# Attention weights of query tiles 3 and 4 normalised behind their exponentials instead of at the slot's end

## The chip, the cores and the metric

The kernel runs on one core of a Trainium2 chip, with float32 inputs and outputs. The metric is the device time of one execution in microseconds (us), measured without the profiler; before the change three runs gave a median of 985.2 us. A change of this kernel can be told from no change when it is over about 0.2%, some 2 us.

## What is computed

Three layers follow each other: causal attention with a memory term, a dense two-layer block, and a mixture of eight experts in which each token goes to one. The change lies in the attention alone:

```
scores = scale * np.matmul(q, k.transpose(0, 1, 3, 2))          # B, H, S, D = 4, 8, 576, 64
scores = np.where(causal, -1000000000.0, scores)
a = np.exp(scores - scores.max(-1, keepdims=True))
a /= a.sum(-1, keepdims=True) + 1e-09
local = np.matmul(a, v)
...
return (g * mem_out + (1 - g) * local).astype(np.float32)
```

The result, 2304 tokens by 512, goes through `(h * clip(h + 3, 0, 6) / 6) @ w_out` with `h = x @ w_in`, and then through the experts.

## The kernel before, in words

**Units of attention.** The 32 heads are worked on as 16 pairs (`Pair`, L261), two heads at a time. The 576 queries of a head are cut into five tiles, 0 to 4, the first of 64 queries and the others of 128; tile i sees 64, 192, 320, 448 or 576 keys. A pair goes through these steps, each a method with a letter:

- B, `start` (L301): VectorE writes the memory term of all tiles into the weights' tiles `a` (L314).
- S, `scores` (L319): TensorE multiplies `qd` and `kd` into PSUM tiles `pa` (L337); VectorE scales, masks and reduces them in one instruction with an accumulator read (L343), which gives `st` and the extreme `mn`. S0 does tiles 0 and 1 and a corner of 4; S2, S3 and S4 do one tile each.
- X, `exp` (L349): ScalarE takes the exponential into `a` and sums it into `sm` (L352), once for each head.
- N, `norm` (L355): VectorE adds up the sums (L360) and inverts them (L361), and GpSimd multiplies the weights by the inverse in place (L365). N0 does tiles 0, 1 and 2 of both heads, six instructions on GpSimd; N3 does tiles 3 and 4, four instructions.
- T, `turn` (L367): TensorE transposes the normalised weights by 128 x 128 blocks into `pa` (L376), and ScalarE (L91) or VectorE (L93) copies them to `aw`. TA and TB turn blocks of tiles 3 and 4, TC blocks of tiles 4, 2 and 1, TD of 0, 1 and 2.
- V, `values` (L381): TensorE multiplies `vt` by `aw` (L389), and ScalarE copies the result into `x`. V3 is tiles 3 and 4, V0 the others.
- M and L are the memory term and the loads of the pair after the next.

The `pa` tiles come from a pool of four PSUM buffers (L245).

**Slots.** `PROGRAM` (L75) is a string that is run 17 times, for t = -1 to 15; one run is a slot (`act`, L427). In slot t, the steps T and V are those of pair t, and B, S, X and N those of pair t + 1, so that one pair is turned while the next is scored. C and D load and convert a piece of the dense block's weights (`load64`, L135: a load of 512 KB, then L150 and L91 on ScalarE, L154, L155, L164 and L166 on VectorE). U asks for the next unit of the dense block (`mlp`, L168), whose matmuls are L213 and L182; there are none before slot 4, when the first 512 tokens are there. From slot 4 the dense block's units fill the slots.

**What sets the order.** Every engine works its instructions in the order in which the program gives them. The program text is not that order: a scheduler takes the instructions and places them on the engines by when it thinks their inputs are there, and, among those that are, by their place in the text. So the position of N3 in `PROGRAM` is a priority, and what becomes of it has to be looked up in the built program.

```
def norm(self, g):
    tiles = GROUPS[g]
    g0, g1 = tiles[0], tiles[-1] + 1
    for j in range(2):
        h, a, r = 2 * self.hp + j, self.a[j], self.rs[j]
        DVE.tensor_reduce(r[:, g0:g1], self.sm[j][:, g0:g1], axis=AX.X, op=ALU.add)
        DVE.reciprocal(r[:, g0:g1], r[:, g0:g1])
        for i in tiles:
            m, n, o = QN[i], QK[i], QO[i]
            av = a[:m, o + D : o + D + n]
            ENG[NORM[i]].tensor_scalar(av, av, r[:m, i], omg[:m, h : h + 1], op0=ALU.mult, op1=ALU.mult)
```

`GROUPS` (L259) is `{0: (0, 1, 2), 3: (3, 4)}`, and `NORM` is GpSimd for all five tiles.

Of the kernel before, what the change touches and what calls it, by code (L numbers as in the profile page):

```python
# [23 lines left out]
B, H, S, D = 4, 8, 576, 64  # L24
# [17 lines left out]
TB = 256  # L42
# [29 lines left out]
ET = {'A': mybir.EngineType.Activation, 'D': mybir.EngineType.DVE, 'P': mybir.EngineType.Pool, 'T': mybir.EngineType.PE}  # L72


PROGRAM = 'B S0 L TA S3 X0 U X3 X1 I U TB S4 C U X4 TC U S2 C X2 N0 M0 TD U M1 V3 N3 M2 D U K U M3 V0 U U'  # L75


def f32(ap):
# [4 lines left out]
def tile_kernel(ctx, tc, qT, kT, qn, vx, z, beta, w_in, w_out, w_gates, w1, w2, out):  # L83
# [343 lines left out]
    def act(t, x):  # L427

        nonlocal it
        pair = lambda n: pairs[n] if 0 <= n < len(pairs) else None  # L430
        k, n = x[0], int(x[1]) if x[1:].isdigit() else None
        cur, nxt, far = pair(t), pair(t + 1), pair(t + 2)
        if k == "U":
            other()
        elif k == "I":
            if t in ready:
                for _ in it:
                    pass
                it = mlp(ready[t], 0, end1)
                other()  # L440
        elif k == "L":
            if far:
                far.load()
        elif k == "K":
            if nxt and nxt is not pairs[0]:
                nxt.load_v()
        elif k in "CD":
            if conv and (k == "C" or t >= 3):
                load64(cv, 0, *conv.pop(0))
        elif k == "B":  # L450
            if nxt:
                nxt.start()
        elif k == "S":
            if nxt:
                nxt.scores(n)
        elif k == "X":
            if nxt:
                nxt.exp(n)
        elif k == "N":
            if nxt:  # L460
                nxt.norm(n)
        elif k == "T":
            if cur:
                cur.turn(x[1])
        elif k == "V":
            if cur:
                cur.values(n)
        elif k == "M":
            if far:
                far.memory(n)  # L470
# [4 lines left out]
    for t in range(-1, len(pairs)):  # L475
        for x in PROGRAM.split():
            act(t, x)
# [742 lines left out]
```

## Time and profile before

| | |
|---|---|
| median of 3 runs | 985.2 us (984.69 to 986.05) |
| the profiled execution | 991.04 us |
| its span, first to last instruction | 989.2 us |
| mean granted clock of TensorE over the span | 0.973 |
| TensorE (PE) busy | 917.4 us, 93% |
| VectorE (DVE) busy | 622.1 us, 63% |
| ScalarE (ACT) busy | 520.3 us, 53% |
| GpSimd (POOL) busy | 367.7 us, 37% |

PE stands for matmuls and PEld for weight loads, which overlap them. A busy share is an average over the whole kernel, and TensorE's matmuls are pipelined, so a full TensorE need not be at its peak. In the timelines a line gives the start, the time, the engine, the line of the kernel, the operation with its output and input, how many were merged, and in brackets the idle time in front of it with what ended it. The granted clock is a share of full speed: 1.00 is 2.4 GHz, 0.50 is 1.2 GHz.

### The profile page before, as it was taken

What the parts mean: (1) busy time and instruction counts of PE and PEld (TensorE: products, weight loads), DVE (VectorE), ACT (ScalarE), POOL (GpSimd) and SP (SyncE); (2) the same over time, 40 slices, a digit from 0 to 9 for tenths busy, and PEclk for the clock granted to TensorE, in tenths of its full rate; (3) what the DMA queues carried; (4) which work ended last, traced back from release to release, by engine and by line L of the source; (5) the groups of instructions that cost most, each with busy time, mean ns of one, the idle gap of its engine ahead of it and who ended that gap; (6) DMA issues with size and microseconds to landing.
All of it is one profiled execution on the core that took longest, in us unless ns stands there. A gap on an engine that the chain in (4) does not pass through costs nothing. (4 is left out here: it accounts for less than half of the span.)

```text
span 989.2 us, 17067 instructions
## 1 busy us (share of the span) xinstructions
PE 917.4 (93%) x5733; PEld 720.5 (73%) x5733; DVE 622.1 (63%) x1511; ACT 520.3 (53%) x1084; POOL 367.7 (37%) x574
## 2 busy tenths in 40 slices
PE   4677799999999999899999999999887999999996
PEld 2344477777776777788888888888766778778875
DVE  6766797565657541778344444447767668678982
ACT  5556666565546543445222222223346668768883
POOL 1543376445546552435533333335221123112210
PEclk9987799999999999989999999999999999999998
DMA  6432332221213010543011111112323565532850
GB/s 196 129 100 95 118 117 71 76 75 54 75 54 100 14 35 17 176 129 128 22 44 44 43 44 43 45 43 107 107 76 118 204 240 190 204 130 104 319 201 23
DMA packets 49278, 101.70 MB, mean 103 GB/s; under 512 B 5341, under 2 KB 15581, under 8 KB 49184
## 3 DMA queue, kind: packets, MB, share of 16 engines
q1 hardware_dynamic: 45696, 89.74, 26.8%
q0 software_dynamic: 3488, 10.80, 3.2%
q8 instruction: 47, 0.77, 0.3%
q14 instruction: 47, 0.39, 0.1%
HBM read 136.66 MB, written 14.72 MB: 153 GB/s over the span
## 5 line engine op out<-in xcount | busy, mean ns | idle before, releaser
L646 DVE TENSOR_TENSOR wL<-st,wH 128x1024 fp32r<-128x1024 f32 x136 | 163.7, 1227 | 43.2 <-ACT wH L641 37.5
L213 PE MATMUL hps<-xH,wH 128*128 128x256 f32 x576 | 166.8, 290 | 1.6 <-ACT xH L91 1.4
L213 PE MATMUL hps<-xL,wH 128*128 128x256 f32 x576 | 162.2, 282 | 2.9 <-DVE xL L200 2.9
L95 POOL TENSOR_SCALAR gH<-g 128x256 fp32r<-128x256 f32 x144 | 63.6, 441 | 271.8 <-DVE g L217 214.4
L365 POOL TENSOR_SCALAR a<-a,rs,omg 128x320 f32<-128x320 f32 (+4 forms) x160 | 126.9, 805 | 97.1 <-DVE rs L360 72.5
L213 PE MATMUL hps<-xH,wL 128*128 128x256 f32 x576 | 161.2, 280 | 0.0
L217 DVE SCALAR_TENSOR_TENSOR g<-g,hps 128x256 f32<-128x256 f32 x144 | 60.0, 417 | 146.4 <-ACT g L216 146.4
L641 ACT CAST wH<-st 128x1024 fp32r<-128x1024 f32 x136 | 139.7, 1053 | 8.5 <-DMA st<-w 8.4
L216 ACT ACTIVATE g<-hps,half 128x256 f32<-128x256 f32 x144 | 68.0, 472 | 137.4 <-PE hps L213 112.3
L213 PEld LDWEIGHTS hps<-xH,wH 128*128 128x128 f32 x576 | 108.9, 189 | 18.6 <-issue 12.6
L221 POOL TENSOR_TENSOR gL<-g,gH 128x256 fp32r<-128x256 f32 x144 | 115.4, 802 | 11.8
L213 PEld LDWEIGHTS hps<-xL,wH 128*128 128x128 f32 x576 | 109.1, 189 | 8.6 <-DVE xL L200 3.8
L352 ACT ACTIVATE a<-st,mn 64x64 f32<-64x64 f32 (+4 forms) x160 | 88.4, 555 | 48.0 <-DVE mn L343 48.0
L376 PE MATMUL pa<-ident,a 128*128 128x128 f32 (+1 forms) x480 | 81.9, 302 | 32.1 <-POOL a L365 28.5
L213 PEld LDWEIGHTS hps<-xH,wL 128*128 128x128 f32 x576 | 109.1, 190 | 0.1
L376 PEld LDWEIGHTS pa<-ident,a 128*128 128x128 f32 (+1 forms) x480 | 59.0, 151 | 60.6 <-POOL a L365 33.8
L182 PE MATMUL acc<-wH,gH 128*128 128x512 f32 x288 | 95.5, 413 | 1.3 <-POOL gH L95 1.2
L182 PE MATMUL acc<-wH,gL 128*128 128x512 f32 x288 | 91.7, 400 | 2.3 <-POOL gL L221 2.3
L337 PE MATMUL pa<-kd,qd 64*128 64x64 f32 (+5 forms) x384 | 83.7, 488 | 10.3 <-DVE mn L343 5.4
L182 PE MATMUL acc<-wL,gH 128*128 128x512 f32 x288 | 91.0, 397 | 0.0
L343 DVE CUSTOM_DVE_ANT_0 st<-pa,mask 64x64 f32<-64x64 f32 (+4 forms) x160 | 52.9, 372 | 33.0 <-PE pa L337 33.0
L182 PEld LDWEIGHTS acc<-wH,gL 128*128 128x128 f32 x288 | 54.2, 190 | 16.2 <-POOL gL L221 3.5
(239 smaller groups left out, 1674.6 us busy)
## 6 DMA issues: line engine op xcount, KB each, us to landing
st<-w SPq DMA_DIRECT2D x136, 512.0 KB
sw<-w SPq DMA_DIRECT2D x32, 512.0 KB
w<-w_in SPq DMA_DIRECT2D x16, 512.0 KB
w<-w_out SPq DMA_DIRECT2D x16, 512.0 KB
qnt<-qn SPq DMA_DIRECT2D x16, 320.0 KB
vt<-vx SPq DMA_DIRECT2D x16, 320.0 KB
x2d<-row SPq DMA_DIRECT2D x18, 258.0 KB
qd<-qT SPq DMA_DIRECT2D x16, 288.0 KB
```

The lines of the kernel that those rows point to most:

```text
L95: POOL.tensor_scalar(out, x, 1.0, 1.0, op0=ALU.mult, op1=ALU.mult)
L182: PE.matmul(acc[t], lhsT=gg[:, t * P : (t + 1) * P], rhs=ww[:, 512:1024], start=m == 0 and first, stop=m == HM - 1 and last)
L213: PE.matmul(hps, lhsT=ww[:, kk * P : (kk + 1) * P], rhs=xx[:, kk], start=k == 0, stop=k == 3 * KD - 1)
L216: ACT.activation(g, hps, AF.Relu, bias=half, scale=1.0 / 6.0)
L217: DVE.scalar_tensor_tensor(g, g, 1.0, hps, op0=ALU.min, op1=ALU.mult)
L221: ENG[GL].tensor_tensor(gL, g, f32(gH), op=ALU.subtract)
L337: PE.matmul(pss[j][: QN[i], o : o + k1 - k0], lhsT=self.qd[r, QS[i] : QS[i] + QN[i]], rhs=self.kd[r, k0:k1], start=True, stop=True)
L352: ACT.activation(self.a[j][:m, o + D : o + D + n], self.st[j][i][:m, :n], AF.Exp, bias=self.mn[j][:m, i : i + 1], scale=-1.0, accum_out=se ...
L365: ENG[NORM[i]].tensor_scalar(av, av, r[:m, i], omg[:m, h : h + 1], op0=ALU.mult, op1=ALU.mult)
L376: PE.transpose(psa[:, off : off + QN[i]], self.a[j][: QN[i], QO[i] + c * P : QO[i] + (c + 1) * P], ident[: QN[i], : QN[i]])
L641: ACT.copy(self.H[c], stage[c])
L646: DVE.tensor_tensor(self.L[c], stage[c], f32(self.H[c]), op=ALU.subtract)
```

## The change

One token of `PROGRAM` moves: N3 stood behind V3, near the slot's end, and now stands behind X4, the exponentials of tile 4, and in front of TC. Nothing is added or removed.

```
-PROGRAM = 'B S0 L TA S3 X0 U X3 X1 I U TB S4 C U X4 TC U S2 C X2 N0 M0 TD U M1 V3 N3 M2 D U K U M3 V0 U U'
+PROGRAM = 'B S0 L TA S3 X0 U X3 X1 I U TB S4 C U X4 N3 TC U S2 C X2 N0 M0 TD U M1 V3 M2 D U K U M3 V0 U U'
```

What the built program makes of it is shown at two places, both in slot 1, in which pair 2 is scored; the later numbers in names tell buffers apart.

On GpSimd, before: `a_464` and `a_465` are the weights of pair 2's two heads, and the memsets prepare the sums of pair 4.

```order
L365 TENSOR_SCALAR a_465<-a_465,rs_471,omg 128x320
L308 MEMSET sm_856 128x10
L308 MEMSET sm_857 128x10
L309 MEMSET sm_856 128x1
L309 MEMSET sm_857 128x1
L365 TENSOR_SCALAR a_464<-a_464,rs_470,omg 128x448
L365 TENSOR_SCALAR a_464<-a_464,rs_470,omg 128x576
L365 TENSOR_SCALAR a_465<-a_465,rs_471,omg 128x448
L365 TENSOR_SCALAR a_465<-a_465,rs_471,omg 128x576
```

GpSimd with the change, the same pair:

```order
L365 TENSOR_SCALAR a_464<-a_464,rs_470,omg 128x448
L365 TENSOR_SCALAR a_464<-a_464,rs_470,omg 128x576
L365 TENSOR_SCALAR a_465<-a_465,rs_471,omg 128x448
L365 TENSOR_SCALAR a_465<-a_465,rs_471,omg 128x576
L308 MEMSET sm_856 128x10
L309 MEMSET sm_856 128x1
L365 TENSOR_SCALAR a_464<-a_464,rs_470,omg 64x64
```

The four instructions of N3 (448 and 576 keys) stood behind the six of N0; now they stand in front of them.

On VectorE, before: `rs` are the inverted sums, 128x3 those of N0 and 128x2 those of N3; `w` and `wL` belong to the conversion of the dense block's weights, `phi` and `pz` to the memory term of pair 3.

```order
L360 TENSOR_REDUCE rs_470<-sm_468 128x3
L93 COPY aw<-pa 128x320
L361 RECIPROCAL rs_470<-rs_470 128x3
L360 TENSOR_REDUCE rs_471<-sm_469 128x3
L292 SCALAR_TENSOR_TENSOR phi<-qnt,phi 128x640
L166 TENSOR_TENSOR wL_555<-w_588,wH_554 128x512
L361 RECIPROCAL rs_471<-rs_471 128x3
L360 TENSOR_REDUCE rs_470<-sm_468 128x2
L360 TENSOR_REDUCE rs_471<-sm_469 128x2
L295 TENSOR_TENSOR pz<-phi,zb 128x10x64
L361 RECIPROCAL rs_470<-rs_470 128x2
L361 RECIPROCAL rs_471<-rs_471 128x2
```

VectorE with the change, from the end of tile 4's scores to the first of tile 2's:

```order
L343 ISA st_483,mn_467<-pa,mask,mn 128x512
L343 ISA mn_467 128x1
L155 SCALAR_TENSOR_TENSOR w_556<-w_556 128x512
L360 TENSOR_REDUCE rs_470<-sm_468 128x2
L154 TENSOR_SCALAR w_596<-w_596 128x512
L164 SCALAR_TENSOR_TENSOR w_556<-w_556 128x512
L361 RECIPROCAL rs_470<-rs_470 128x2
L360 TENSOR_REDUCE rs_471<-sm_469 128x2
L93 COPY aw<-pa 128x512
L361 RECIPROCAL rs_471<-rs_471 128x2
L343 ISA st,mn_466<-pa,mask 128x320
L343 ISA mn_466 128x1
```

The sums of N3 were added up and inverted behind those of N0 and all scores of the slot; now this happens between the scores of tile 4 and those of tile 2, in between the steps of a weight conversion. TensorE's order is the same but for single matmuls of the dense block in slot 0. From slot 5 on, the orders of all engines are the same before and after, and there N3 stands in front of N0 in both.

## Rows read from the trace of the kernel before

**Rows 1.** The page: the span, and busy time of each engine.

```profile
span 989.2 us, 17067 instructions
PE 917.4 (93%) x5733; PEld 720.5 (73%) x5733; DVE 622.1 (63%) x1511; ACT 520.3 (53%) x1084; POOL 367.7 (37%) x574
```

**Rows 2.** Waits of PE, 0 to 125 us: us in total, times, longest.

```profile
PE pa L376 <- POOL a L365: 26.9, 17, 7.2
```

**Rows 3.** Waits of PE, 120 to 400 us: the same wait.

```profile
PE pa L376 <- POOL a L365: 1.6, 2, 0.9
```

**Rows 4.** Slots 0, 2, 5-15: length; PE, PEld, DVE, ACT, POOL busy; clock; DMA; GB/s.

```profile
28.90:49.70 20.80, 16.14 (x87) 9.21 (x87) 15.02 (x52) 12.51 (x32) 9.18 (x15) 1.00 0.34 114
...
71.03:92.02 20.99, 15.46 (x87) 8.90 (x87) 15.05 (x53) 13.25 (x34) 8.16 (x15) 0.84 0.35 114
...
140.00:400.00 260.00, 257.94 (x1755) 194.38 (x1754) 151.47 (x509) 142.07 (x390) 135.54 (x235) 1.00 0.20 63
```

**Rows 5.** Timeline of PE, end of slot 1 and most of slot 2.

```profile
66.34 1.02 PE L337 MATMUL pa<-kd,qd 64*64 64x64 f32 x12
71.03 0.33 PE L376 MATMUL pa<-ident,a 128*128 128x128 f32 x1 [3.67 <-POOL a L365]
71.84 1.17 PE L376 MATMUL pa<-ident,a 128*128 128x128 f32 x4 [0.48 <-POOL a L365]
73.34 0.90 PE L376 MATMUL pa<-ident,a 128*128 128x128 f32 x3 [0.33 <-POOL a L365]
74.17 1.87 PE L337 MATMUL pa<-kd,qd 64*128 64x448 f32 x4
75.97 1.97 PE L376 MATMUL pa<-ident,a 128*128 128x128 f32 x8
77.87 1.58 PE L337 MATMUL pa<-kd,qd 64*128 64x512 f32 x4
79.38 1.10 PE L376 MATMUL pa<-ident,a 128*128 128x128 f32 x8
```

**Rows 6.** Timeline of POOL: N0 and N3 of slot 1, N3 of slots 4 and 8.

```profile
65.20 4.72 POOL L365 TENSOR_SCALAR a<-a,rs,omg 64x64 f32<-64x64 f32 x6 [13.21 <-DVE rs L360]
...
70.14 3.15 POOL L365 TENSOR_SCALAR a<-a,rs,omg 128x448 f32<-128x448 f32 x4
...
140.39 4.75 POOL L365 TENSOR_SCALAR a<-a,rs,omg 128x448 f32<-128x448 f32 x4
...
222.41 3.03 POOL L365 TENSOR_SCALAR a<-a,rs,omg 128x448 f32<-128x448 f32 x4 [1.34 <-DVE rs L361]
```

**Rows 7.** Timeline of DVE: its long waits in slots 0, 2 and 4, and tile 4's scores in slot 8.

```profile
29.93 0.43 DVE L154 TENSOR_SCALAR w<-w 128x512 int32<-128x512 int32 x1 [0.63 <-DMA w<-w_out]
35.06 0.62 DVE L343 CUSTOM_DVE_ANT_0 st<-pa,mask 128x448 f32<-128x448 f32 x1 [4.09 <-PE pa L337]
...
76.07 0.62 DVE L343 CUSTOM_DVE_ANT_0 st<-pa,mask 128x448 f32<-128x448 f32 x1 [4.98 <-PE pa L337]
79.48 0.75 DVE L343 CUSTOM_DVE_ANT_0 st<-pa,mask,mn 128x512 f32<-128x512 f32 x1 [0.96 <-PE pa L337]
...
118.39 0.69 DVE L166 TENSOR_TENSOR wL<-w,wH 128x512 fp32r<-128x512 f32 x1 [4.88 <-ACT wH L91]
...
220.15 0.75 DVE L343 CUSTOM_DVE_ANT_0 st<-pa,mask,mn 128x512 f32<-128x512 f32 x1 [0.47 <-PE pa L337]
```

**Rows 8.** Waits of DVE, 195 to 400 us: its wait for the sums of ACT's exponentials.

```profile
DVE rs L360 <- ACT a L352: 5.5, 17, 0.4
```

**Rows 9.** One line's instructions, L155 on DVE: duration ns min/median/max, first and last start.

```profile
L155 DVE SCALAR_TENSOR_TENSOR w<-w x17: 681/692/1218, 18.8 to 399.8; 128x512 int32<-128x512 int32 x17
```

**Rows 10.** Waits of ACT, 0 to 125 us: its wait for the dense block's first weights.

```profile
ACT w L150 <- DMA w<-w_in: 5.1, 6, 2.7
```

**Rows 11.** Busy time by stretch, slot 2: from S3 to S4, and behind them.

```profile
74.20:78.00 3.80, 3.80 (x15) 2.18 (x14) 1.93 (x6) 3.17 (x10) 0.00 (x0) 0.50 0.00 0
80.00:88.00 8.00, 7.02 (x59) 4.33 (x57) 8.00 (x24) 5.68 (x15) 1.90 (x2) 1.00 0.49 145
```

## The prediction

> **What bounds the kernel now.** First the page: TensorE is busy for 917.4 of 989.2 us [rows 1], so the question is where its missing time lies. The waits of PE answer for the attention: in the first 125 us it waits 26.9 us, 17 times, for L365, the normalising on GpSimd, in front of the transposes [rows 2]; from 120 to 400 us the same wait is 1.6 us [rows 3]. The table by stretch shows why: from 140 us on TensorE is busy 257.94 of 260 us, because units of the dense block stand between the attention steps, while in slots 0 to 3 there are none, and no engine is full [rows 4].
>
> The timelines of slots 1 and 2 show the ring these early slots run in. TensorE ends S0 at 67.36 (66.34 + 1.02) and then has TA, which needs N3 [rows 5]. GpSimd is at N0 from 65.20 for 4.72 us, and N3 stands behind it, from 70.14 [rows 6]. So TA starts at 71.03, after 3.67 us of idle time, and then runs in step with N3. The scores S3 stand behind TA on TensorE and start at 74.17 [rows 5]; VectorE, out of work, waits 4.98 us for them, until 76.07 [rows 7]. Only then come tile 4's and tile 2's scores, their exponentials, N0, and N3 again. The slot takes 20.99 us, of which VectorE works 15.05 and TensorE 15.46 [rows 4].
>
> **The change part by part.** No instruction is added or removed, and no DMA is issued in addition. In slots -1 to 4 the four instructions of N3 go ahead of the six of N0 on GpSimd, and its two sums and two inversions on VectorE go ahead of tile 2's scores; the loads on SP's queue change places only among themselves. From slot 5 on the orders are the same, so nothing is gained or lost in the eleven slots where the dense block runs, except the start of slot 5, whose TA still waits for slot 4's N3: those are the 1.6 us [rows 3].
>
> *What goes.* In a slot whose order already is the new one, N3 starts 2.26 us after tile 4's scores start on VectorE (222.41 less 220.15) [rows 6, 7]. In slot 2 that is 79.48 + 2.26 = 81.7, and it ends by 84.8 to 86.5, with its 3.03 to 4.75 us [rows 6, 7]. S0 of that slot ends on TensorE about one slot of 20.99 us behind the 67.36, at 88.4; TA no longer waits for GpSimd. But TensorE's wait isn't the gain: what it stops delaying is VectorE, which has the least slack behind it. TA without its waits can start at 67.4 instead of 71.03, 3.7 us earlier, and loses the two pauses inside it, 0.8 us together, so S3 ends about 4.5 us earlier, near 71.6, where VectorE is ready at 71.1 (76.07 less 4.98). I therefore count VectorE's long wait as gone: 4.98 us in each of slots 1 to 3 (one of three equal rows stands), 4.09 and 0.63 in slot 0, where the small one is a load that has more time to land [rows 7]. In slot 4 the long wait has another name, 4.88 us for a ScalarE cast, L91 [rows 7], but that cast stands in ScalarE's queue behind the copies of TA, so it goes too.
>
> *What is late next.* VectorE, with 15.05 us of work in a slot of 20.99 [rows 4]. Three costs are put on it.
> - The sums of N3 now stand on VectorE right behind tile 4's scores and wait for ScalarE; tile 2's scores are queued behind them, and TensorE's TD and ScalarE's next exponentials wait for those. Slots 7 to 14 show this wait: 5.5 us in 17 times, 0.32 each [rows 8]. Two a slot, 0.65 us; at least nothing, as conversion steps stand between them here.
> - N3 now runs beside VectorE's conversion steps. L155 takes 692 ns in the median and up to 1218 [rows 9], and N3 itself 3.03 to 4.75 us [rows 6]: the long ones are those in which both engines work on SBUF. I take 0.75 us a slot, one and a half such stretches of 0.5 us; the bounds are nothing and 1.8 us, all of L155 and L164 of two conversions, four at 0.45.
> - The wait for tile 4's scores, 0.96 us [rows 7], stays as it is; at best it goes too.
>
> The second cost has a rule behind it. The Trainium skill, GPSIMD Engine Reference, section 1 (Specifications), says that GpSimd shares its SBUF interfaces with VectorE and that the two contend when VectorE's instruction has two SBUF inputs, as L155 and L164 do. By that rule every conversion step under N3 would be stretched, which is the upper bound of 1.8 us; the trace agrees that there are two durations, but in the median the step is at the short one.
>
> *The sum.* 0.65 + 0.75 = 1.4 us a slot. Slot 0: 4.72 - 1.4 = 3.3. Slots 1 to 3: 3 x (4.98 - 1.4) = 10.7. Slot 4: 4.88 - 0.65 = 4.2, since there its N3 lies among the dense block's units, whose slack covers the stretching. Start of slot 5: 1.6. Together 19.8 us. Everything behind slot 5 only starts earlier: TensorE is full there [rows 4], and no later load or wait of the program is tied to a clock time. The profiled execution took 991.0 us and would take 971.2; the median of the runs shown is 5.8 us below it, and the same sum gives 985.2 - 19.8 = **965.4 us**.
>
> Its own bounds: with no cost at all and the 0.96 us of four slots gained too, 19.8 + 6.2 + 3.8 = 29.8 us, 955; with 0.65 + 1.8 = 2.45 us in all five slots and nothing at slot 5, 2.3 + 7.6 + 2.4 = 12.3 us, 973.
>
> **The rivals.**
> - *TensorE's wait is gained in full.* If TensorE, not VectorE, is what the slot waits for, the whole 26.9 + 1.6 = 28.5 us go: 956.7. For it: without the idle time in front of TA its clock need not fall. From S3 to S4 the granted clock is 0.50, later in the slot 1.00 [rows 11], and eight transposes take 1.97 us there and 1.10 later [rows 5]. Against it: VectorE's 15.05 us would have to fit without a pause. The Trainium skill, TensorE: Matmul & The Clock Gate, Part 1, says that the default clock is the lower one and sustained activity releases it; the fall behind the idle time agrees. By that rule alone TA to S4 would lose a good part of their 7.8 us, a gain on TensorE that VectorE's work hides.
> - *A load takes the wait's place.* ScalarE's L150, the first step of a conversion, stands in front of the copies of TA, and it waits for its load 5.1 us in six times, 2.7 at most [rows 10]. With shorter slots the same bytes come in less time. At 2.7 us in each of slots 0 to 3, 10.8 us are given back: 985.2 - 9.0 = 976. Against it: the loads take a third of the DMA engines' time [rows 4].
> - *Slower: TensorE stays at the lower clock.* If the now even, half-loaded stream keeps TensorE at 1.2 GHz through the whole slot, its 15.46 us grow: 7.8 us (TA 2.4, S3 1.87, TB 1.97, S4 1.58 [rows 5]) are slow already, the other 7.7 double, 23.1 us with about 1 us of pauses on top, 24.1 against 20.99. It decides as soon as TensorE's work in a slot exceeds 21 us. Four slots lose 12.4, slots 4 and 5 gain 5.8: 991.8. Against it: in slot 2 the granted clock is back at 1.00 from 80 us on [rows 11].
> - *No change.* If TA's operands were not the last thing S3 waits for, S3 would stay where it is: 985.
>
> **How the numbers follow.** The forecast 0.70; the full wait 0.12; the load 0.10; the slower clock 0.04; no change 0.04. The range takes the forecast's own bounds and the first rival, 956 to 973, and leaves out the other three, 0.18. Faster by over 0.2%, which is about what a measurement can tell here: 0.70 + 0.12 + 0.10 = 0.92. Within 0.2%: 0.04. Slower: 0.04.
>
> **What would show it.** Right: in the waits of PE over the first 125 us, L376 behind L365 falls from 26.9 us to under 3; VectorE's waits for L337 in front of tile 3's scores fall from 4.98 us to under 1; the slots, read between the first transposes of TA, take 17 to 18 us instead of 21; the sums L360 show waits of about 0.3 us; the stretch from slot 5 to the end keeps its length within 2 us. Wrong, step by step: a slot of 17 us and an unchanged total would mean that something behind slot 5 is tied to time; S3 that starts late behind ScalarE's copies or L150 would mean the load; slots of 15 us that VectorE costs nothing; a granted clock of 0.5 through the slots the slower rival; a wait of TC for N0, which is now the later of the two, a new one that I hold to be covered by the 8 us from TA to TC.

## The result, and the profile after

The changed kernel took 973.1 us in the median of four runs (971.3 to 975.5) beside 985.6 us for the kernel before: a ratio of 0.9874, 95% interval 0.985 to 0.9898. Two more comparisons, told below, gave 973.8 beside 987.7 (0.9851; 0.9822 to 0.9879) and 972.1 beside 987.7 (0.9838; 0.9812 to 0.9864). The gain is 12.5 to 15.6 us: real, but less than the 19.8 us that were forecast, and 973.1 lies just above the range, 972.1 inside it. Two executions, one of 2982 us of the kernel before and one of 2183 us of a variant below, stand apart and are in no ratio.

First the page of the kernel after, against [rows 1]: the span, the busy time of all engines, and the granted clock in 40 slices.

```profile
span 973.4 us, 17053 instructions
PE 915.6 (94%) x5733; PEld 721.7 (74%) x5733; DVE 627.7 (64%) x1511; ACT 519.3 (53%) x1084; POOL 370.5 (38%) x574
PEclk9989899999999999899999999999999999999998
```

The work is the same, and VectorE needs 5.6 us more for it. The waits of PE over the first 125 us, against [rows 2]:

```profile
PE pa L376 <- DVE mn L343: 8.0, 8, 3.2
PE pa L337 <- DVE mn L343: 5.1, 2, 4.6
...
PE pa L376 <- POOL a L365: 3.0, 3, 1.3
```

The wait that the change was to take away is gone, 26.9 us down to 3.0, and those 3.0 stand in slot 0. A third of it has come back under another name: the same transposes wait 8.0 us in eight times for L343, VectorE's reading of the scores, which frees the PSUM buffers that they need. (The wait of L337 stood there before the change too, with 5.0 us.) The table by stretch, from the first transposes of TA of one slot to those of the next, slots 1 to 5 and the rest, against [rows 4] (length; PE, PEld, DVE, ACT, POOL busy; clock; DMA):

```profile
46.54:62.51 15.97, 14.56 (x91) 8.76 (x89) 14.94 (x48) 12.62 (x34) 8.65 (x16) 0.89 0.40 135
62.51:80.93 18.42, 14.67 (x88) 8.70 (x86) 16.98 (x56) 13.23 (x36) 8.99 (x13) 0.91 0.45 142
80.93:96.85 15.92, 14.27 (x88) 8.40 (x86) 14.94 (x48) 12.38 (x34) 8.65 (x16) 0.89 0.40 135
96.85:125.84 28.99, 25.53 (x164) 18.73 (x162) 27.57 (x74) 17.70 (x45) 17.54 (x23) 0.88 0.48 145
125.84:155.57 29.73, 26.54 (x172) 20.34 (x171) 24.33 (x68) 16.67 (x44) 17.43 (x27) 0.94 0.25 74
155.57:973.40 817.83, 790.22 (x5021) 639.91 (x5019) 496.18 (x1113) 420.96 (x829) 291.44 (x443) 0.99 0.29 99
```

Slots 1 to 3 take 16 to 18.4 us in place of 21 to 22, and VectorE fills all but 1.0 to 1.4 us of each. Slots 4 and 5 are not shorter than the 28.3 and 26.7 us of the first trace of before, but longer, and in slot 4 VectorE works 27.57 of 28.99 us.

The gain can be followed along the program at the same instruction, the first transpose of TA. The table sets two traces of the kernel before (the second is told below) against three of the changed one, in us from the start; the last column is the difference of the means, the one before it the prediction's sum of whole slots up to there (the 1.6 us of the start of slot 5 fall inside its TA, behind this first transpose).

| TA of slot | before, two traces | after, three traces | forecast gain | gain |
|---|---|---|---|---|
| 1 | 49.7, 48.9 | 46.5, 46.7, 46.7 | 3.3 | 2.7 |
| 2 | 71.0, 70.0 | 62.5, 62.7, 62.6 | 6.9 | 7.9 |
| 3 | 92.0, 90.8 | 80.9, 81.2, 81.1 | 10.5 | 10.3 |
| 4 | 114.0, 112.2 | 96.9, 95.6, 97.0 | 14.0 | 16.6 |
| 5 | 142.3, 140.9 | 125.8, 125.7, 126.0 | 18.2 | 15.8 |
| 6 | 169.0, 172.1 | 155.6, 156.1, 155.7 | 19.8 | 14.7 |

Up to slot 4 the change brings 2.6 us more than forecast. In slots 4 and 5, where another 5.8 us were to come, 1.9 us are lost between the means. (That is a miss of 7.7 us there. Part of it and of the 2.6 is a matter of booking: the wait for N3 that goes with slot 4's term, 5.0 us, stands in front of TA of slot 4 and so in the length of slot 3. Booked there, the forecast up to slot 4 is 18.2 us, of which 1.6 are missing, and the two slots bring a loss of 1.9 in place of a gain of 1.6. The 5.1 us that are missing at slot 6 do not hang on the booking.) The 14.7 us that are left at slot 6 agree with the 12.5 to 15.6 us of the medians. Two places on PE's timeline show where: TA and the next two steps of slot 4, then TA, S3 and a matmul of the dense block in slot 5.

```profile
96.85 1.09 PE L376 MATMUL pa<-ident,a 128*128 128x128 f32 x8
98.18 1.50 PE L337 MATMUL pa<-kd,qd 64*128 64x448 f32 x4 [0.24 <-ACT aw L91]
102.91 1.97 PE L376 MATMUL pa<-ident,a 128*128 128x128 f32 x8 [3.22 <-DVE mn L343]
...
125.84 1.09 PE L376 MATMUL pa<-ident,a 128*128 128x128 f32 x8
130.13 1.63 PE L337 MATMUL pa<-kd,qd 64*128 64x448 f32 x4 [3.19 <-DVE mn L343]
...
132.45 0.41 PE L213 MATMUL hps<-xH,wH 128*128 128x256 f32 x1
```

TA takes 1.09 us without a pause, so N3 is in time. Then TB waits 3.22 us, and a slot later S3 waits 3.19 us, both for VectorE's L343. Behind the waits the eight transposes take 1.97 us, and the dense block's matmul 0.41 us; in slot 4, from 108 us on, such a matmul takes 0.28. The granted clock is 0.50 there, from 101.1 to 107.8 and from 131.8 to 135.1 us: it fell once during and once behind a wait. VectorE's timeline of slot 4 says why L343 is late:

```profile
97.08 0.79 DVE L295 TENSOR_TENSOR pz<-phi,zb 128x640 f32<-128x640 f32 x1
97.79 0.41 DVE L154 TENSOR_SCALAR w<-w 128x512 int32<-128x512 int32 x1
98.13 0.81 DVE L298 TENSOR_REDUCE rn<-pz 128x10 f32<-128x650 f32 x1
98.87 0.79 DVE L155 SCALAR_TENSOR_TENSOR w<-w 128x512 int32<-128x512 int32 x1
...
99.70 0.81 DVE L164 SCALAR_TENSOR_TENSOR w<-w 128x512 int32<-128x512 int32 x1
100.43 1.00 DVE L314 SCALAR_TENSOR_TENSOR a<-phi,gt,rn 128x192 f32<-128x192 f32 x3
101.35 0.68 DVE L166 TENSOR_TENSOR wL<-w,wH 128x512 fp32r<-128x512 f32 x1
101.95 0.34 DVE L314 SCALAR_TENSOR_TENSOR a<-phi,gt,rn 128x128 f32<-128x128 f32 x1
102.22 0.20 DVE L343 CUSTOM_DVE_ANT_0 st<-pa,mask 64x64 f32<-64x64 f32 x1
```

Not one pause: when TensorE has S0's scores ready, VectorE is still 5 us deep in the memory term and in the third weight conversion of slot 3 (D, which is there from slot 3 on). With N3 in the way this backlog was worked off while TensorE waited. The same two slots of the kernel before, in its first trace, show how little TensorE had left to gain there:

```profile
113.98:142.30 28.32, 27.41 (x163) 19.20 (x163) 22.97 (x66) 16.88 (x43) 14.40 (x21) 0.84 0.35 104
142.30:168.98 26.68, 24.98 (x172) 18.65 (x171) 22.11 (x64) 16.83 (x44) 19.61 (x29) 1.00 0.27 84
```

TensorE is busy for all but 2.6 us of the two. VectorE works 22.97 us in slot 4, 4.6 us less than after the change. The theory that went into the experiments is therefore: **VectorE's backlog at the start of slots 4 and 5 takes the place of the wait for N3.** Its rivals: N3's new place in slot 4 costs the time itself; N3 on GpSimd stretches VectorE's instructions; TensorE at its lower clock is the bound there.

Slot 0 hides something of the kind behind a good number. Its TA starts at 21.4 to 21.6 us in place of 28.6 and 28.9, since the wait in front of it, 7.1 us, is gone; but then the slot takes 25.1 us in place of 20.8 and 20.3, with VectorE at work for 20.8 of them in place of 15.0 [rows 4], as work that it had done during the wait now falls behind it:

```profile
21.39:46.55 25.16, 18.00 (x88) 9.99 (x87) 20.79 (x62) 13.86 (x35) 15.58 (x23) 1.00 0.37 112
```

### The profile page after: what moved, and what is told of

The parts are those of the page before. It is cut to its first block, busy times and chain, and to the rows that moved or that the text cites. A ratio compares the mean times of both kernels' runs of the same rounds, so it can differ in the third digit from the quotient of the medians.

```text
span 973.4 us, 17053 instructions
## 1 busy us (share of the span) xinstructions
PE 915.6 (94%) x5733; PEld 721.7 (74%) x5733; DVE 627.7 (64%) x1511; ACT 519.3 (53%) x1084; POOL 370.5 (38%) x574
## 5 line engine op out<-in xcount | busy, mean ns | idle before, releaser
L365 POOL TENSOR_SCALAR a<-a,rs,omg 128x320 f32<-128x320 f32 (+4 forms) x160 | 128.1, 812 | 78.0 <-DVE rs L360 52.1
L337 PE MATMUL pa<-kd,qd 64*128 64x64 f32 (+5 forms) x384 | 82.1, 470 | 13.8 <-DVE mn L343 8.7
L376 PE MATMUL pa<-ident,a 128*128 128x128 f32 (+1 forms) x480 | 75.3, 289 | 13.3 <-DVE mn L343 8.0
L376 PEld LDWEIGHTS pa<-ident,a 128*128 128x128 f32 (+1 forms) x480 | 55.6, 145 | 37.1 <-DVE mn L343 14.0
L708 POOL DMA_INDIRECT out<-ys,idxs x17 | 19.2, 1128 | 124.7 <-ACT ys L707 69.4
L182 PEld LDWEIGHTS acc<-wH,gL 128*128 128x128 f32 x288 | 54.3, 190 | 15.9 <-POOL gL L221 3.1
```

The costliest lines, as they stand in the source:

```text
L182: PE.matmul(acc[t], lhsT=gg[:, t * P : (t + 1) * P], rhs=ww[:, 512:1024], start=m == 0 and first, stop=m == HM - 1 and last)
L337: PE.matmul(pss[j][: QN[i], o : o + k1 - k0], lhsT=self.qd[r, QS[i] : QS[i] + QN[i]], rhs=self.kd[r, k0:k1], start=True, stop=True)
L376: PE.transpose(psa[:, off : off + QN[i]], self.a[j][: QN[i], QO[i] + c * P : QO[i] + (c + 1) * P], ident[: QN[i], : QN[i]])
```

## The experiments

All edits are to the changed kernel unless the kernel before is named. Where an experiment leaves work out, other values reach the choice of experts and the part behind attention changes its length, so it is read up to TA of slot 6 alone.

**What repeats.** The changed kernel twice more, unedited, and the kernel before once more.

> The changed kernel once more, beside the three variants, on the chip that runs them. By every theory the measured gain repeats: 971 to 975 us, 0.985 to 0.990 of the kernel before. If its trace shows the dense part behind slot 5 at the same length as the kernel before (within 1 us), the 2 us between 386 and 440 us in the first comparison were the phase of the clock; if the 2 us appear again at the same place, they are the change's.

> The changed kernel a third time, for the spread of its trace and as the measure of the next two. 971 to 975 us; TA of slot 4 at 95 to 97 us, of slot 6 at 155 to 157; the waits of TB in slot 4 and of S3 in slot 5 for VectorE 3 us each again.

> The kernel before, profiled once more: what its trace gives when nothing is changed. Theory: up to 386 us (the end of attention) the starts repeat within 1 us (TA of slot 4 at 114, of slot 6 at 169, the last at 388); between 386 and 440 us, where the first trace of before lost 2 to 4 us against each variant, it moves by that much, as the phase of the clock. If it repeats there within 0.5 us, those microseconds belong to the change.

The two times are those above. Both traces of the changed kernel have the waits of 3.2 us again, in front of TB in slot 4 and of S3 in slot 5. The kernel before did not repeat within 1 us: TA of slot 4 came at 112.2 (1.8 us earlier) and of slot 6 at 172.1 (3.1 us later), because its slot 5 took 31.2 us in place of 26.7. Table by stretch of that second trace, slots 4 and 5:

```profile
112.16:140.89 28.73, 27.61 (x163) 19.23 (x163) 23.65 (x67) 16.91 (x43) 14.67 (x22) 0.83 0.32 101
140.89:172.05 31.16, 28.50 (x172) 21.01 (x170) 24.35 (x67) 16.89 (x44) 18.26 (x28) 0.89 0.23 72
```

The granted clock is 0.89 in a slot that had 1.00 in the first trace, and TensorE waits 2.1 us for L343 there too. So the prediction's base held a lucky slot 5; in the two kernels without the change that are told below the granted clock of slot 5 is 0.89 and 0.88 too. Behind slot 6 the three traces of the changed kernel take 817.8, 812.4 and 812.3 us, with 22.4, 7.0 and 6.7 us of the lower clock in them, the two of the kernel before 820.2 and 819.1 with 22.9 and 22.8. So most of the difference goes with the clock; at an equal share of the lower clock the changed kernel is still 1.2 to 2.4 us shorter there, and whether these are the 2 us that the expectation asks about, and the change's, stays open.

**N3's place in slot 4.** Slots from 4 on use the old order:

```diff
-        for x in PROGRAM.split():
+        for x in (PROGRAM if t < 4 else LATE).split():
```

> The changed order in slots -1 to 3 only; slot 4, where the dense block begins, has N3 at its old place. Theory (in slot 4 VectorE is full, with a third weight conversion and the dense block's first units, and moving N3 there neither gains nor loses much): within 1.5 us of the changed kernel, 971 to 975; the wait for N3 in front of TA at the start of slot 5 is back, 1 to 2 us, and slot 4 is shorter by as much. Rival (N3 among the dense units stretches VectorE in slot 4 and is itself what loses the 3.7 us): 3 to 5 us faster than the changed kernel, 967 to 970.

971.9 us, ratio 0.9828 (0.9797 to 0.986), beside 973.8 on the same chip. TA of slots 4 to 6 takes 58.8 us as in the changed kernel. Waits of PE in that stretch:

```profile
PE pa L379 <- DVE mn L346: 3.2, 1, 3.2
PE pa L379 <- POOL a L368: 1.2, 2, 1.0
PE pa L340 <- DVE mn L346: 0.5, 1, 0.5
```

(Lines stand three further down.) TB's wait is the same 3.2 us, so N3's move in slot 4 doesn't cause it. S3's 3.2 us fell to 0.5, and the wait for N3 came back with 1.2 us; TensorE's idle time fell, but slot 5 had 0.89 of the clock in place of 0.94. The rival's 967 to 970 did not come; the change's part in slot 4 is worth nothing that these runs can tell.

**Less work on VectorE.** The third conversion of slots 3 and 4 without its three bit operations, in both kernels:

```diff
+        if light:
+            lo = hi
-        if SIGN == "D":
+        elif SIGN == "D":
...
-            load64(cv, 0, *conv.pop(0))
+            load64(cv, 0, *conv.pop(0), light=k == 'D')
```

> The changed kernel; the third conversion of slots 3 and 4 leaves out its three bit operations on VectorE (L154, L155, L164) and takes the high words as they are, so that two of the 16 weight pieces are wrong; its cast, its subtraction and its load stay. That takes 2 x 2.3 us of VectorE's work out of slots 3 and 4, and nothing from any other engine. Theory (VectorE's backlog of slots 3 and 4 is what eats the gain there): 3 to 5 us faster than the changed kernel, 968 to 970, and the waits of 3.22 us in front of TB in slot 4 and of 3.19 us in front of S3 in slot 5 fall under 1.5 us each. Rival (TensorE bounds slot 4, 25.5 us busy of 29.0): within 1 us of the changed kernel.

> The kernel before with the same work left out (three bit operations on VectorE of the third conversion in slots 3 and 4; two of the 16 weight pieces are wrong). Theory: there N3's wait set slots 3 and 4 and VectorE had 6 us of idle time in slot 4, so taking 4.6 us from it brings less than 1.5 us: 984 to 986. Then the change, measured between the two light kernels, gains 15 to 18 us in place of 12.5. Rival (VectorE's load in slots 3 and 4 was the bound before the change too): 3 to 5 us faster than the kernel before, 981 to 983.

TA of slot 6 came at 153.2 in place of 155.6 to 156.1, a gain of 2.4 to 2.9 where 3 to 5 were expected, and in the kernel before at 172.5, no gain; the two light kernels are 19.3 us apart there, a little over the 15 to 18 expected. By their medians, 1066.8 and 1076.2 us, they are only 9.3 us apart: behind slot 6 their traces take 909.4 and 903.9 us, with 38.9 and 32.4 us of the lower clock. TB's wait fell to 1.3 us and S3's for VectorE to 0.5, but S3 now waited 2.3 us for L91, ScalarE's copy of the transposes. So VectorE's work set these waits, and another engine stands close behind it.

Then the whole third conversion left out of slots 3 and 4 (two weight pieces filled with zeros), in both kernels:

```diff
+        if skip:
+            POOL.memset(f32(hh), 0.0)
+            POOL.memset(f32(ll), 0.0)
+            return
```

> The changed kernel without the third conversion of slots 3 and 4: two weight pieces are set to nothing by two fills on GpSimd each, so that in either slot 3.1 us of VectorE's work, 1.35 us of ScalarE's and a load are gone. To be read up to TA of slot 6, since other values change what follows. Theory (the conversions on VectorE and ScalarE together bound slots 4 and 5): the waits of TB in slot 4 and S3 in slot 5 fall under 1.5 us each with no new one over 1.5, and TA of slot 4 to TA of slot 6 takes 53 to 56 us in place of 58.7 to 60.5. Rival (TensorE with its lower clock behind S0 and its four score buffers bound them whatever VectorE and ScalarE do): 57 us or more.

> The kernel before with the same conversions left out; to be read up to TA of slot 6. Theory: its slots 0 to 4 wait for N3 and not for conversions, so TA of slot 4 stays at 111 to 114 us, and TA of slot 6 comes at most 2 us earlier than in the two traces of the kernel before (169.0 and 172.1): 167 to 171. Then the change between the two kernels without these conversions gains 17 us or more at TA of slot 6, against 13 to 16 with them. Rival: it gains as much as the changed kernel does from the same cut, and the difference stays at 13 to 16.

Tables by stretch, slots 4 and 5, of the changed kernel without these conversions, and of the kernel before without them:

```profile
98.05:124.20 26.15, 25.07 (x165) 18.08 (x163) 25.16 (x72) 16.67 (x44) 16.54 (x25) 0.93 0.45 139
124.20:153.31 29.11, 26.53 (x172) 20.31 (x171) 21.61 (x62) 15.19 (x42) 15.33 (x25) 0.94 0.20 59
```

```profile
110.11:137.90 27.79, 26.99 (x163) 18.91 (x163) 21.25 (x56) 16.98 (x41) 17.12 (x23) 0.88 0.30 92
137.90:167.40 29.50, 28.13 (x173) 21.01 (x171) 20.09 (x60) 14.54 (x41) 17.15 (x27) 0.88 0.21 58
```

The changed kernel needs 55.3 us for the two slots in place of 58.7 to 60.5 (59.3 on the mean of three traces), the kernel before 57.3 us, between its two traces of 55.0 and 59.9 (57.4 on the mean). Of the 4.0 us that the cut brings in the changed kernel, 3.1 are idle time of TensorE, 3.7 us in place of 6.8; in the kernel before it brings nothing that its spread lets one tell. On the means, 3.9 of the 7.7 us by which these slots missed the forecast (5.8 + 1.9) go with the third conversions. With one trace of either kernel and 4.9 us between the two traces of the kernel before, that share is rough; that the cut helps the changed kernel is clear of its spread. TB's wait fell to 0.8 us, as the theory has it; S3's only to 2.6 where under 1.5 was expected. At TA of slot 6 the two kernels are 14.1 us apart, not the 17 expected, since TA of slot 4 moved as well: 3 us earlier in one, 1.6 us later in the other, whose slot 2 had 10.2 us at the lower clock.

The same work at another time, the third conversion in slots 1 and 2:

```diff
-            if conv and (k == "C" or t >= 3):
+            if conv and (k == "C" or t in (1, 2)):
```

> The changed kernel with the third weight conversion in slots 1 and 2, not in 3 and 4: the same work, two slots earlier. Theory A (the change made VectorE the bound of all of slots 1 to 5, its idle time there under 1.5 us a slot): what leaves slots 3 and 4 is paid in 1 and 2, and the time stays within 1.5 us of the changed kernel, 971 to 975, TA of slot 6 at 155 to 157 us. Theory B (only slots 4 and 5 are overfull): the waits of 3.2 us in front of TB of slot 4 and S3 of slot 5 go and nothing takes their place: 967 to 970, TA of slot 6 at 150 to 152.

976.97 us, ratio 0.9905 (0.988 to 0.9931): some 3 to 5 us slower than the changed kernel's medians, though not timed beside it, and both theories missed. TA of slots 4 to 6 did fall to 54.6 us, slot 4 with full clock and no wait of TensorE over 0.5 us,

```profile
103.96:128.32 24.36, 23.88 (x164) 17.83 (x162) 24.19 (x68) 15.98 (x43) 17.14 (x26) 1.00 0.42 139
```

while S3 of slot 5 still waited 2.4 us for L343. But slots 2 and 3 rose to 21.1 and 20.3 us, from 18.4 and 15.9, with 13.6 us of the lower clock in them in place of 6.8. In these slots a third conversion cost 7.1 us and saved 4.7 later; how much of the cost is the clock's was not taken apart.

**N3 beside VectorE.** N3's multiplications left out everywhere, then for three pairs alone:

```diff
-                for i in tiles:
+                for i in tiles if g == 0 else ():
```

> The changed kernel without N3's four multiplications on GpSimd, so that tiles 3 and 4 stay unnormalised; its sums and inversions stay. To be read up to TA of slot 6, since other values change what follows. It asks what the multiplications cost VectorE by running beside it: VectorE's busy time over the whole kernel rose by 5.6 us from the kernel before to the changed one. Theory S (this stretch is the missing 4 to 6 us): VectorE's L154, L155, L164, L166 and L314 fall to their short durations, and TA of slot 6 starts at 150 to 152 us in place of 155.6. Theory B (the order and amount of VectorE's work at the start of slots 4 and 5, stretched or not): waits of 2 us or more in front of TB of slot 4 and S3 of slot 5 stay, and TA of slot 6 starts at 153 to 156.

> The changed kernel without N3's multiplications on GpSimd in slots 3, 4 and 5 alone (tiles 3 and 4 of three pairs stay unnormalised; to be read up to TA of slot 6). Theory S (they stretch VectorE in slots 4 and 5, and that is what lost the gain there): up to TA of slot 3 as the changed kernel (80 to 82 us); from TA of slot 4 to TA of slot 6 it takes 55 to 57 us in place of 58.7 and 60.5, and the waits of 3.2 us fall under 2. Theory B (order): that stretch keeps 58 us or more and the waits of 3 us.

The steps of the conversion on VectorE by line (busy us, mean ns of one; idle before): of the kernel before from 29 to 142 us, of the changed one from 21 to 125, and of the one without N3's multiplications from 21 to 120.

```profile
L155 DVE SCALAR_TENSOR_TENSOR w<-w 128x512 int32<-128x512 int32 x12 | 9.2, 787 | 0.0
L164 DVE SCALAR_TENSOR_TENSOR w<-w 128x512 int32<-128x512 int32 x12 | 8.9, 741 | 0.0
L166 DVE TENSOR_TENSOR wL<-w,wH 128x512 fp32r<-128x512 f32 x12 | 8.2, 687 | 4.9 <-ACT wH L91 4.9
L154 DVE TENSOR_SCALAR w<-w 128x512 int32<-128x512 int32 x13 | 5.5, 449 | 0.8 <-DMA w<-w_out 0.6
```

```profile
L166 DVE TENSOR_TENSOR wL<-w,wH 128x512 fp32r<-128x512 f32 x14 | 12.8, 912 | 4.4 <-ACT wH L91 4.1
L164 DVE SCALAR_TENSOR_TENSOR w<-w 128x512 int32<-128x512 int32 x13 | 11.4, 877 | 0.0
L155 DVE SCALAR_TENSOR_TENSOR w<-w 128x512 int32<-128x512 int32 x13 | 9.9, 758 | 0.0
L154 DVE TENSOR_SCALAR w<-w 128x512 int32<-128x512 int32 x13 | 6.8, 538 | 0.0
```

```profile
L166 DVE TENSOR_TENSOR wL<-w,wH 128x512 fp32r<-128x512 f32 x14 | 11.0, 787 | 2.4 <-ACT wH L91 2.1
L164 DVE SCALAR_TENSOR_TENSOR w<-w 128x512 int32<-128x512 int32 x13 | 9.4, 727 | 0.0
L155 DVE SCALAR_TENSOR_TENSOR w<-w 128x512 int32<-128x512 int32 x13 | 9.3, 718 | 0.0
L154 DVE TENSOR_SCALAR w<-w 128x512 int32<-128x512 int32 x13 | 6.0, 475 | 0.0
```

The four means of a conversion add up to 2.66, 3.09 and 2.71 us: the stretch is 0.42 us a conversion, two a slot, three with D. Without N3's multiplications at all, TA of slot 6 starts at 147.1, earlier than either theory had it and 8.7 us ahead of the changed kernel, 3.5 of them up to TA of slot 1; slots 4 and 5 take 55.2 us, with waits of 2.6 and 1.5 us in front of TB and S3. Without those of slots 3 to 5 alone, slots 4 and 5 take 57.7 us and keep waits of 2.8 and 2.5 us: 1.6 us less than the 59.3, between what the two theories named, and nearer to theory B (order and amount). So N3 beside VectorE within these two slots is the smaller part of the loss. The 2.5 us more that the first edit brings there would be a smaller backlog from the slots before; with one trace of either that is not shown.

**Another order, another engine.** L314 behind S0's scores, or behind tile 4's; TB's copy on ScalarE; these together; and L166 on GpSimd.

```diff
-PROGRAM = 'B S0 L TA S3 X0 U X3 X1 I U TB S4 C U X4 N3 TC
+PROGRAM = 'B S0 G L TA S3 X0 U X3 X1 I U TB S4 C U X4 N3 TC
+PROGRAM = 'B S0 L TA S3 X0 U X3 X1 I U TB S4 C U X4 G N3 TC
...
-TURN = [dict(A='A', B='D',
+TURN = [dict(A='A', B='A',
...
-CONV_L = 'D'
+CONV_L = 'P'
```

(One of the two new orders at a time; G is L314.)

> The changed kernel with the four multiplications of the memory term (L314, 2.1 us a slot, up to 3.6 where stretched), which stand ahead of S0's scores on VectorE, right behind them; nothing is taken away. Theory (S0's scores come late on VectorE, and TB and S3 wait for the buffers that they hold): TB's wait of 3.2 us in slot 4 falls to 1 to 2 and S3's in slot 5 to 0 to 1; 2 to 4 us faster than the changed kernel, 969 to 971. Rival (VectorE's total work bounds slots 1 to 5, whatever its order): within 1 us of the changed kernel.

> The same four multiplications moved further, behind tile 4's scores and exponentials, ahead of N3's sums. Theory (S0 and then S3 and S4 are what TensorE's buffers and ScalarE's exponentials wait for): 2 to 5 us faster than the changed kernel, 968 to 971, at least as good as right behind S0. Rival (total work): within 1 us. A loss would be N3's sums coming 2 us later behind them, so that TA waits for GpSimd again.

> The changed kernel with one copy of TB a slot (0.67 us on VectorE) on ScalarE. Theory A (VectorE bounds slots 1 to 5): 0.67 us a slot in five or six slots, 3 to 4 us faster, 969 to 970. Rival (ScalarE, 12.4 of 16 us busy in those slots and with a wait of 2.3 us behind its copy in the kernel with less VectorE work, is as near to the bound): within 1 us of the changed kernel, or slower.

> The last edit together with TB's copy on ScalarE (one copy of 0.67 us a slot off VectorE, which alone gave 970.2). If both relieve VectorE at the start of slots 4 and 5, the gains add up: 966 to 969, and TA of slot 6 at 150 to 153. If they remove the same wait, 968 to 970.

> L314 right behind S0's scores, and one copy of TB a slot on ScalarE: the two edits that were each 1 to 3 us faster than the changed kernel. If VectorE's lateness in front of S0 and its load both count: 966 to 969, with the upper end of its interval against the kernel before under the changed kernel's 0.985. If the two gains are the same one or noise: 969 to 972.

> The fastest version so far (L314 behind tile 4's scores, one copy of TB on ScalarE) once more, on another chip: 967 to 970 us and a ratio of 0.978 to 0.983 if it is faster than the changed kernel (0.984 to 0.987 in three comparisons); 0.984 or more if the first time was a draw.

> The changed kernel with the subtraction of each weight conversion (L166, 0.67 to 1.27 us, two or three a slot up to slot 5) on GpSimd in place of VectorE. Theory A (VectorE bounds slots 1 to 5): some 0.85 us for each of about 13 subtractions behind slot 0 go from the bound, against about 1.6 us each on GpSimd (its subtraction of half the size takes 0.80), which is half idle there: 4 to 9 us faster than the changed kernel, 964 to 969. Rival (GpSimd's N0 and N3 become late by the 3 us a slot that it gets more, and TA and TC wait again): as the changed kernel or up to 8 us slower.

| edit | us, median | ratio to before, 95% |
|---|---|---|
| L314 behind S0 | 971.6 | 0.983 (0.9789 to 0.9871) |
| L314 behind S4 | 975.1 | 0.986 (0.9817 to 0.9903) |
| TB's copy on ScalarE | 970.2 | 0.9841 (0.9817 to 0.9865) |
| L314 behind S4, TB's copy | 969.3 | 0.9805 (0.9771 to 0.9838) |
| the same once more | 971.7 | 0.9812 (0.9788 to 0.9837) |
| L314 behind S0, TB's copy | 974.0 | 0.9852 (0.9823 to 0.9881) |
| L166 on GpSimd | 985.5 | 0.998 (0.9961 to 0.9999) |

Neither the order alone nor the copy alone changes anything that can be told from the changed kernel's 0.984 to 0.987. L314 behind S4 (968 to 971 by its theory) and L314 behind S0 with the copy (972 at most) came out slower than expected. L314 behind S4 with TB's copy on ScalarE came out at 0.981 on two chips, some 4 us faster than the changed kernel; the intervals still touch, and the two were never timed on the same chip, so it is likely but not shown to be better. Its TA of slot 6 lies at 150.3 and 152.4, 3.4 to 5.5 us ahead of the changed kernel's mean; 2.1 to 3.8 us of that stand at slot 4 already. Its slots 4 and 5 take 57.6 and 58.1 us. L314 behind S0 together with that copy shows why single cures bring little. Waits of PE from TA of slot 4 to that of slot 6:

```profile
PE pa L340 <- ACT aw L91: 3.1, 2, 2.9
PE pa L379 <- DVE mn L346: 1.6, 2, 1.4
```

The wait for VectorE is gone from S3 (L340 here), and one of 2.9 us for ScalarE's copy stands there; the two slots take 58.3 us. And L166 on GpSimd, half idle as it looked, lost nearly all of the gain. The instruction there, and the longest wait of PE up to slot 6:

```profile
L166 POOL TENSOR_TENSOR wL<-w,wH 128x512 fp32r<-128x512 f32 x16 | 24.0, 1499 | 1.5 <-ACT wH L91 1.5
```

```profile
PE pa L337 <- ACT aw L91: 14.8, 5, 6.9
```

The subtractions take 1.50 us each and stand in one queue with N0 and N3. ScalarE waits 12.9 us in five times for loads of `w_in` in front of L150, the next conversions' first step, and the copies of the transposes stand behind L150 in its queue: a conversion that ends later frees its buffer later. That chain is read from the waits and was not tried by itself. The loss of 12 us is larger than the 8 that the rival was given.

## Why the prediction was wrong

- **The wait removed, and slots 1 to 3: right.** L376 behind L365 fell from 26.9 to 3.0 us (under 3 was named), all of them in slot 0; slots took 16.0, 18.4 and 15.9 us (17 to 18 named; 16.8 on the mean), VectorE's waits for tile 3's scores 1.5 us at most (under 1 named). TA of slot 4 gained 16.6 us where 14.0 were forecast.
- **The costs in these slots.** The 0.65 us of waiting for the sums did not come: L360 waits for nothing up to 125 us. The stretch of 0.75 us a slot came, as two times 0.42. A gain that was not in the sum came with it: up to TA of slot 4 the profile shows the lower clock for 21.5 and 21.0 us before and 10.2, 6.8 and 10.2 after, which is the argument for the first rival, that TensorE's clock need not fall in front of TA. So that the sum came out near there is in part luck. Slot 0's 3.3 us against the 2.7 measured are luck: its TA came 7.2 us earlier and the slot then grew by 4.5 us (both on the means), and of VectorE's waits there, 4.72 us that the sum took as gone, 4.4 are there again, 2.9 of them now for ScalarE's cast L91.
- **The step that failed** is "Slot 4: 4.88 - 0.65 = 4.2, since there its N3 lies among the dense block's units, whose slack covers the stretching. Start of slot 5: 1.6." These 5.8 us became a loss of 1.9 on the means; even against the slower trace of the kernel before it is a gain of no more than 1.2 us. The step booked a wait of VectorE as time gained, without a row of TensorE in these slots. There TensorE had only 2.6 us of idle time left in the first trace and 3.8 in the second, less than the 5.8; the rest of its time was work, in part at the lower clock. In the changed kernel its idle time there is 6.7, 7.1 and 6.7 us, nearly all of it two new waits. The 4.88 us wait for the cast did go, but it was also the time in which VectorE caught up. With it gone, VectorE has 27.57 us of work in 28.99, S0's scores are late, and TensorE waits 3.2 us at TB and 3.2 us at S3: the very test that the prediction applied to slots 1 to 3, "what is late next", was not applied to slots 4 and 5, where D, issued in slots 3 and 4, adds 3.1 us of VectorE's work each time. Without those conversions the two slots gain 2.0 us (57.3 against 55.3, one trace each) in place of losing 1.9.
- **The rest of that step is open in its cause.** Some 3.8 us of the miss stay without the third conversions. What the time is spent on can be read: where the full clock was granted for a whole slot, TensorE was busy for 23.9 to 24.0 us in slot 4 and 24.5 to 25.0 us in slot 5 (three traces each), 48.4 to 49.0 us together. The changed kernel's 52.0 to 53.4 us of busy time hold 3 to 5 us that the lower clock adds, behind the two waits; with the 6.7 to 7.1 us of idle time that makes its 58.7 to 60.5. The lower clock was no smaller before (52.4 and 56.1 us busy), so it explains the length of the slots and their spread, not the loss. Less stretch, another order and less VectorE work each left 55 to 59 us for the two slots, with a wait for ScalarE's copies or L343 that moved from TB to S3. That the four score buffers, which either engine has to empty, tie the three engines together fits all of it, but more buffers were not tried.
- **Everything behind slot 5 only starts earlier: right** within what the clock leaves. Slots 6 on take 820.2 and 819.1 us before and 817.8, 812.4 and 812.3 after, with the times at the lower clock as unequal; at an equal time, the first of the three, they are 1.2 to 2.4 us shorter where 2 were named.
- **The other rivals.** The load did not take the place: L150 waits 3.7 us in four times, 1.3 at most, less than in [rows 10]; TensorE did not stay at the lower clock; the time did change. Of the upper bound for the stretch, 1.8 us a slot, the runs show about half, 0.84: on the mean L164 rose from 741 to 877 ns, L166 from 687 to 912 and L154 from 449 to 538, L155 did not (787 to 758). The Trainium skill, GPSIMD Engine Reference, section 1 (Specifications), says that GpSimd's SBUF interfaces are shared with VectorE and that it contends with VectorE's instructions in a 2-port perf mode or with two SBUF inputs. L164 and L166, with two such inputs, agree with that; L155, which has two as well, does not on the mean, and in which mode the one-input L154 runs no run here shows.

## What to carry to other kernels

A wait that is removed also served the engines that were waiting behind it: for each slot that it shortens, compare every engine's work with the new length, above all in the slots that carry extra work, and not only in the typical one. Look up, in each slot for which a gain is booked, how much idle time the engine that ends the slot has there: a wait of another engine cannot by itself give back more. Where several engines empty the same few buffers, relieving the one that is waited for can show the next at once (3.2 us behind VectorE became 2.3 to 2.9 us behind ScalarE here), so the gain of a single cure is bounded by the second-latest. And take a second profile of the kernel before: one trace's slot can be 4.5 us shorter than the next one's.

## What was not expected of the hardware

The lower clock is granted in different places in different executions of one program. The kernel before had 1.00 in slot 5 in one trace and 0.89 in the next (26.7 and 31.2 us), and the changed kernel's part behind attention had 22.4, 7.0 and 6.7 us of it in three traces. Its executions lie between 983.5 and 993.8 us before and 970.1 and 975.5 after, mostly with the longer time at the lower mean clock (before: 983.5 at 0.979, 991.2 at 0.973).

GpSimd and VectorE slow each other: with N3 beside it a conversion took 0.42 us longer on VectorE, and N3's four multiplications took 3.9, 4.4 and 3.9 us in slots 1 to 3 where they had taken 3.15 beside a VectorE that mostly waited [rows 6, 7]. A subtraction of 128x512 took 1.50 us on GpSimd, and 0.68 us on VectorE where nothing stretched it.
